# V of batch 3 issued in another pass, the last output tile in two column halves, and a reordered front and first pass, in a chunked attention followed by a snake MLP

## The chip, the cores and the metric

The kernel runs on one core of a Trainium2 chip. The metric is the device time in microseconds of one execution. All work is on that core's engines: PE (TensorE), ACT (ScalarE), DVE (VectorE), POOL (GpSimd) and SP (SyncE), which here only issues DMAs.

## The reference, cut to what matters

Four batches, eight heads, 768 positions, head size 64. Attention is done in chunks of 32 positions, each of which sees 8 memory keys, 16 positions to its left and 8 to its right. The result of all heads is a matrix of 3072 rows and 512 columns, which goes through an MLP with a "snake" in the middle.

```python
# attention, for each chunk c of 32 positions
k_full = concat(mem_k, k[l_start:r_end]);  v_full = concat(mem_v, v[l_start:r_end])
a = softmax(q_c @ k_full.T / sqrt(64));    out[c] = a @ v_full
# MLP on x = out as [3072, 512];  w_in [512, 2048], w_out [2048, 512]
h = x @ w_in
g = h + sin(alpha * h) ** 2 / (alpha + 1e-9)
return g @ w_out
```

## The kernel before, in words

The order of all work is written out by hand; no scheduler moves anything. Each engine has one queue and works through it in the order in which the code issued it.

One batch is a pass of three steps. **Attention** works on eight blocks of 96 positions. `scores` multiplies queries by keys (L283) into a pair of PSUM banks and takes the exponential on ACT (L296). `values` multiplies by V (L309) and divides by the sum on DVE (L315, L316), which gives `x_blk`. The blocks are transposed into `xT`, the first five by DMA on SP's queue (L492), the rest on PE (L326, L329). **`layer`** is the first matrix product: for each of 16 slices `ft` of the hidden width, PE multiplies `w_in` by `xT` (L508, two halves of 384 columns), ACT takes the sine (L528), the square is done by ACT (L532), DVE or POOL (L535) as the letter of a string says (A, V, P), and DVE forms `gT` (L538), which frees the pair of banks. `finish` of a slice is emitted one slice later, or two for a P. **`second`** is the product with `w_out` (L554) into one bank for each 128 rows; `end_o` copies the bank to `o_sb` (two buffers), on DVE (L567) or ACT (L569), and SP sends it out (L570). `second` of one batch is a generator; `feed.take(n)` puts n of its matmuls between the instructions of the next batch's attention and layer. What is left at the end runs alone.

Batches 0 and 1 bring K and Q through PE transposes. For batches 2 and 3, `load_rows(b)` issues 22 DMAs on POOL's queue (L143, L148, L153) that bring rows of K and Q to `kst` and `qst`, with a cast; then SP copies the memory keys (L157) and issues 14 DMA transposes (`cross_steps`, L164 and L167) into `kT` and `qT`. In the layer of batch 1 the rows of batch 2 are loaded, all at its start, behind a small POOL copy that waits for `xT` (`gate`, L719); its 14 transposes stand on SP's queue right behind. In the layer of batch 2 the rows of batch 3 are loaded (gate at L726), and the transposes are issued one for each slice. `load_v(b)` brings V of a batch with two or three POOL DMAs (L183, L200) to one of two buffers `vws`. `send_memv` adds the memory values by SP (L210).

The first attention (`attention_first`) is cut otherwise: by pairs of heads `hp` and halves of the positions. `sc_half` is the scores of one unit (L341 adds the mask, L349 multiplies, L356 exponentiates), `pv` its values (L368, then L374 and L375 on DVE), `x` the transpose to `xT` (L385 on PE, L388 copies on ACT). `warm(n)` issues n matmuls on a tile of zeros (L336) whose result nobody reads; they are written to the bank that the next `x` will use, so they wait for the copy of L388 that read it last. `ahead` begins the first half of slices 0 to 2. At the end of each attention `preload_act_table` makes ACT load the sine's table before it is needed (L460 in the first attention).

Two rules of the order matter for the change. PSUM bank pairs are handed out in a ring: in the first attention `plan(big=(4, 0, 2))` names three pairs, taken in turn by `pv` and `sc_half`; who takes a pair waits for the reader of the one before. And every POOL DMA waits for the one eight before it.

Of the kernel before, what the change touches and what calls it, by code (L numbers as in the profile page):

```python
# [9 lines left out]
P = 128  # L10
# [4 lines left out]
F32 = mybir.dt.float32  # L15
ACTF = mybir.ActivationFunctionType
# [26 lines left out]
def kernel(  # L43
# [12 lines left out]
    nc = tc.nc  # L56
    B, H, S, D = q.shape
    NM = mem_k.shape[2]
    d_model, d_ff = moe_w_in.shape
# [3 lines left out]
    FT = d_ff // P  # L63
    KT = d_model // P
    NSUB = S // P
# [7 lines left out]
    mlp = ctx.enter_context(tc.tile_pool(name="mlp", bufs=3))  # L73
# [4 lines left out]
    ps = psum.tile([P, 8, 512], F32, name="ps")  # L78
# [6 lines left out]
    kept = set()  # L85
# [37 lines left out]
    w_out_sb = consts.tile([P, FT, d_model], BF, name="w_out_sb")  # L123
# [53 lines left out]
    def load_v(b, parts=((0, H),)):  # L177
        vw = vws[b % 2][:].rearrange("p h j c -> p (h j) c")
        flat = v.rearrange("b h s d -> (b h s) d")

        def part(p0, p1, first, c0, c1):
            r0 = S * H * b + QW * c0 + first
            nc.gpsimd.dma_start(  # L183
                vw[p0:p1, c0:c1, 0:D],
                flat[r0:r0 + QW * (c1 - c0)].rearrange("(n t) d -> t n d", t=QW)[0:p1 - p0],
            )

        for h0, h1 in parts:
            c0, c1 = h0 * NJ, h1 * NJ
            if b == 0 and h0 == 0:  # L190
                part(16, 64, 0, 0, 1)
                c0 = 1
            part(0, 64, -16, c0, c1)
            c0, end = h0 * NJ, 0
            if b == B - 1 and h1 == H:
                c1 -= 1
                end = 1
            part(72, 128, 48, c0, c1)
            if end:
                nc.gpsimd.dma_start(vw[72:120, c1, 0:D], flat[B * H * S - 48:B * H * S])  # L200
# [132 lines left out]
    def warm(n):  # L333
        z = ps[:, rings["one"][0], :]
        for _ in range(n):
            nc.tensor.matmul(z, idle[:, 0:P], idle[:])  # L336
# [55 lines left out]
    def attention_first(kq, alphas, ahead):  # L392
        xT = xp.tile([P, KT, S], BF, name="xT")
        pt, xb = {}, {}

        def turn_k(hp):
            t = turn(kq[0], hp, None)
            put_k(0, hp, t)
            put_k_edges(0, hp, t)

        def turn_q(hp):
            put_q(0, hp, turn(kq[1], hp, None))

        def sc_half(hp, half):
            pt[hp, half] = unit_scores(hp, half)

        def sc(hp):
            for half in range(2):
                sc_half(hp, half)

        def pv(*u):
            xb[u] = unit_values(*u, pt[u])

        def x(*u):
            unit_turn(xT, *u, xb.pop(u))

        turn_k(0)
        warm(2)
        turn_q(0)
        mt = packed(single(), HP, 32)  # L420
        for g in range(HP):
            nc.tensor.transpose(mt[:, g, :], memk_bf[0:32, 2 * g:2 * g + 2, :].rearrange("p e d -> p (e d)"), ident[0:32, 0:32])
        nc.vector.tensor_copy(memkT[:], mt)
        put_memk(0)
        warm(3)
        turn_k(1)
        put_memv(0, nc.vector, 0, H)
        warm(2)
        sc(0)
        turn_q(1)  # L430
        alphas()
        warm(3)
        sc(1)
        t2 = turn(kq[0], 2, None)
        put_k(0, 2, t2)
        pv(0, 0)
        put_k_edges(0, 2, t2)
        turn_q(2)
        warm(1)
        pv(0, 1)  # L440
        t3 = turn(kq[0], 3, None)
        put_k(0, 3, t3)
        warm(1)
        x(0, 0)
        sc_half(2, 0)
        put_k_edges(0, 3, t3)
        turn_q(3)
        sc_half(2, 1)
        x(0, 1)
        warm(1)  # L450
        plan(big=(4, 0, 2))
        pv(1, 0)
        sc(3)
        units = [(hp, half) for hp in range(1, HP - 1) for half in range(2)]
        for n in range(1, len(units)):
            pv(*units[n])
            warm(1)
            x(*units[n - 1])
            if n == 1:
                nc.scalar.preload_act_table(ACTF.Sin)  # L460
            warm(1)
        warm(1)
        pv(3, 0)
        x(2, 1)
        pv(3, 1)
        x(3, 0)
        ahead(0, 0, xT)
        ahead(1, 0, xT)
        x(3, 1)
        ahead(2, 0, xT)  # L470
        return xT
# [73 lines left out]
    def second(i, gT, cut=0):  # L545

        def begin_o():
            bank = take_bank("one")
            kept.add(bank)
            return bank  # L550

        def part(s, bank, f0, f1):
            for ft in range(f0, f1):
                nc.tensor.matmul(  # L554
                    ps[:, bank, :], gT[:, ft, P * s:P * s + P], w_out_sb[:, ft, :],
                    start=(ft == 0), stop=(ft == FT - 1),
                )
                if ft < FT - 1:
                    yield

        def end_o(s, bank):
            kept.remove(bank)
            rings["one"].remove(bank)
            rings["one"].append(bank)
            o_sb = mlp.tile([P, d_model], F32, name="o_sb", bufs=2)
            if s % 2 == 0 or state["attending"]:
                nc.vector.tensor_copy(o_sb[:], ps[:, bank, :])  # L567
            else:
                nc.scalar.copy(o_sb[:], ps[:, bank, :])  # L569
            nc.sync.dma_start(out[S * i + P * s:S * i + P * s + P, :], o_sb[:])  # L570

        early = []
        if cut:
            for s in range(2):
                early.append(begin_o())
                yield from part(s, early[s], 0, cut)
        for s in range(NSUB):
            bank = early[s] if s < len(early) else begin_o()
            yield from part(s, bank, cut if s < len(early) else 0, FT)
            end_o(s, bank)  # L580
            yield
# [78 lines left out]
    def layer(i, xT, squares, begin, to_feed):  # L660
        gT = gTs[i % 2]
        pend = []
        fed = 0
        for ft in range(FT):
            begin(ft)
            square = squares[ft % len(squares)]
            squared, fin = first(ft, xT, gT, square, begun.pop(ft, None))
            want = to_feed * (ft + 1) // FT
            feed.take(want - fed)
            fed = want  # L670
            for due, f in [p for p in pend if p[0] <= ft]:
                f()
            pend = [p for p in pend if p[0] > ft]
            squared()
            pend.append((ft + (2 if square == "P" else 1), fin))
        for due, f in pend:
            f()
        feed.add(second(i, gT, 0 if i else 13), NSUB * FT)
# [3 lines left out]
    def begin_0(ft):  # L682
        if ft == 3:
            plan(h=[6] + rings["big"])
        if ft == 11:
            load_v(1)
            send_memv(1)
            send_memv(2)
        if ft == 15:
            prs.extend(pair_up(kq1[n // HP], n % HP) for n in range(4))  # L690

    layer(0, xT, "VPPAPAVPPAPAVAAA", begin_0, 0)
    last4 = rings["h"]
    plan(one=(last4[0], last4[0] + 1), t=(last4[1], last4[1] + 1), big=last4[1:])
    put_memk(1)
# [17 lines left out]
    for i in range(1, B):  # L713
        last = i == B - 1
        crossings = iter(()) if last else cross_steps(i + 1)

        def begin(ft, i=i):
            if i == 1 and ft == 0:
                nc.gpsimd.tensor_copy(gate[:], xT[0:1, 0, QW * 6 - 1:QW * 6])  # L719
                load_rows(2)  # L720
                load_v(3)
                for _ in crossings:
                    pass
            if i == 2:
                if ft == 0:
                    nc.gpsimd.tensor_copy(gate[:], xT[0:1, 0, QW * 6 - 1:QW * 6])  # L726
                    load_rows(3)
                if ft >= 1:
                    next(crossings, None)

        if i == 1:
            assert feed.left() == 16
            plan(h=[min(rings["one"])] + rings["big"])
            layer(i, xT, "VAVAVAVAAVAAVAVA", begin, 0)
            free = rings["h"]
            plan(one=(free[0], free[0] + 1), h=free[1:])
        else:
            plan(h=rings["big"])
            layer(i, xT, "AAAV", begin, feed.left() - (0 if last else 16))
        if not last:  # L740
            plan(big=rings["h"])
            nc.scalar.preload_act_table(ACTF.Exp)
            feed.take(6)
            xT = attention(i + 1, feed, (4, 8, 4, 4, 3, 3, 3, 3, 4, 4, 4), 2, 5)
            if i == 1:
                send_memv(3)
# [31 lines left out]
```

## Time and profile before

| what | value |
|---|---|
| median of 11 runs | 225.65 us (224.01 to 227.31) |
| profiled execution, its own time | 225.86 us |
| its span, first to last instruction | 224.1 us |
| PE busy | 209.1 us, 93% of the span |
| ACT busy, DVE busy, POOL busy | 148.0, 136.0, 82.5 us |
| L554 (`w_out`), one matmul of 512 columns x362 | 94.7 us busy |
| L508 (`w_in`), one matmul of 384 columns x512 | 91.4 us busy |
| granted TensorE clock, mean | 0.997 |

The times in the tables and rows are microseconds from the start of the span; the execution's own time is 1.76 us longer than its span. A row of the timeline gives start, length, engine, line, operation, tiles and, in brackets, the idle time of the engine just before with what ended it. "PEld" is the load of weights, which runs beside PE. "SPq" and "POOLq" are the queues of those engines. A busy PE is not PE at its peak, since the ends of matmuls are modelled.

The stages of the span, by their first rows: first attention to 25.7, layer of batch 0 to 48.2, keys and queries of batch 1 to 60.3, attention of batch 1 to 74.2, its layer to 97.8, attention of batch 2 from 99.2 to 115.8, its layer to 149, attention of batch 3 from 149.2 to 162.9, its layer to 197.7, and the rest of `second` to 219.2.

### The profile page before, as it was taken

To read this page: it belongs to the slowest core of one execution; us is meant where nothing else is said; L and a number is where in the kernel's file an instruction comes from. 1 tells how busy PE (TensorE), PEld (TensorE's weight loads), DVE (VectorE), ACT (ScalarE), POOL (GpSimd) and SP (SyncE) were. 2 spreads that over 40 slices of the span, in tenths; PEclk is the share of its full clock that TensorE was granted. 3 is DMA by queue.
4 is the path that set the end of the run, shared out by engine and by line. 5 is a ranking of instruction groups with operands and counts; after the bars stand their busy time and mean duration, and the time that the engine had idled before them with its cause. 6 is when DMAs were issued, how large, how long until landed. Compare 5 with 4: busy or idle time off the path is not lost.

```text
span 224.1 us, 4352 instructions
## 1 busy us (share of the span) xinstructions
PE 209.1 (93%) x1647; PEld 112.5 (50%) x1672; DVE 136.0 (61%) x233; ACT 148.0 (66%) x217; POOL 82.5 (37%) x102
## 2 busy tenths in 40 slices
PE   7999799999999989999599999999999999999991
PEld 2555555545545545544255555544555555544440
DVE  5866559793437689995563875765845754851110
ACT  2558578994778399998645879797918777741001
POOL 8997663795600799900039960000000000000000
PEclk9999999999999999999999999999999999999998
DMA  5999999999999699999969999642410110112121
GB/s 81 160 170 173 207 207 207 200 173 124 105 174 163 67 170 145 157 156 137 161 110 139 132 109 217 139 119 67 115 52 0 47 50 1 47 47 75 69 94 48
DMA packets 98733, 26.96 MB, mean 120 GB/s; under 512 B 86792, under 2 KB 95640, under 8 KB 98712
## 3 DMA queue, kind: packets, MB, share of 16 engines
q0 software_dynamic: 71520, 14.82, 84.5%
q1 hardware_dynamic: 27192, 11.86, 25.9%
q8 instruction: 13, 0.21, 0.4%
q14 instruction: 8, 0.07, 0.1%
HBM read 29.69 MB, written 6.29 MB: 161 GB/s over the span
## 4 chain that ended last, share of the span: by engine, by line
PE 62%; DMA 10%; POOL 8%; SPq 6%; DVE 5%; ACT 4%; issue 3%; DVEq 0%; ACTq 0%; POOLq 0%
PE ps L554 32%; PE ps L508 23%; DMA kT<-kst 5%; DMA q_bf<-in_q_dram 3%; SPq L164 3%; SPq L167 3%; PE ps L283 2%; DMA qst<-in_q_dram 2%; PE ps L309 2%; DVE gT L538 2%; ACT u L528 2%; POOL kst L148 2%; POOL kst L143 1%; POOL qst L153 1%; POOL vw L183 1%
## 5 line engine op out<-in xcount | busy, mean ns | idle before, releaser
L554 PE MATMUL ps<-w_out_sb,gT 128*128 128x512 bf16 x362 | 94.7, 380 | 1.2
L508 PE MATMUL ps<-xT,w_in_sb 128*128 128x384 bf16 x512 | 91.4, 326 | 2.0 <-DVE gT L538 1.3
L538 DVE SCALAR_TENSOR_TENSOR gT<-u,inv_alpha,ps 128x768 bf16<-128x768 f32 x64 | 63.3, 1012 | 24.1 <-ACT u L532 20.1
L528 ACT ACTIVATE u<-ps,alpha_sb 128x768 f32<-128x768 f32 x64 | 56.7, 896 | 26.7 <-PE ps L508 25.8
L508 PEld LDWEIGHTS <-w_in_sb 128*128 128x128 bf16 x512 | 49.5, 97 | 39.8 <-issue 4.2
L554 PEld LDWEIGHTS <-gT 128*128 128x128 bf16 x384 | 34.3, 97 | 31.4 <-issue 0.9
L532 ACT ACTIVATE u<-u 128x768 f32<-128x768 f32 x40 | 33.7, 843 | 1.3
L296 ACT ACTIVATE pt<-ps,biasm 128x256 bf16<-128x256 f32 x72 | 28.7, 473 | 7.2 <-issue 2.8
L567 DVE COPY o_sb<-ps 128x512 f32<-128x512 f32 x17 | 11.7, 689 | 25.3 <-PE ps L554 24.7
L535 DVE TENSOR_TENSOR u<-u 128x768 f32<-128x768 f32 x18 | 17.2, 953 | 6.0 <-ACT u L528 5.9
L183 POOL DMA_DIRECT2D vw<-in_v_dram x15 | 18.1, 1216 | 0.0
L316 DVE TENSOR_TENSOR x_blk<-ps,rinv 96x512 bf16<-96x512 f32 x24 | 16.5, 686 | 1.1 <-DVE rinv L315 0.3
L569 ACT COPY o_sb<-ps 128x512 f32<-128x512 f32 x7 | 4.1, 584 | 19.0 <-PE ps L554 19.0
L262 ACT COPY kT<-ps 128x672 bf16<-128x672 bf16 x8 | 5.7, 718 | 10.0 <-PE ps L247 5.2
L148 POOL DMA_DIRECT2D kst<-in_k_dram x16 | 11.7, 732 | 0.0
L283 PEld LDWEIGHTS <-kT 64*128 64x128 bf16 x192 | 4.9, 94 | 13.0 <-issue 11.3
L143 POOL DMA_DIRECT2D kst<-in_k_dram x16 | 11.2, 699 | 0.3 <-issue 0.3
L315 DVE RECIPROCAL rinv<-ps 96x8 f32<-96x8 f32 x24 | 4.8, 202 | 10.6 <-PE ps L309 5.4
L336 PE MATMUL ps<-idle 128*128 128x512 bf16 x28 | 9.6, 446 | 1.8 <-DVE vw L596 1.2
L309 PEld LDWEIGHTS <-pt 128*128 128x128 bf16 x192 | 9.0, 98 | 4.1
L283 PE MATMUL ps<-qT,kT 64*128 64x96 bf16 x192 | 8.3, 205 | 3.0 <-DVE o_sb L567 1.3
L153 POOL DMA_DIRECT2D qst<-in_q_dram x12 | 10.8, 903 | 0.0
(77 smaller groups left out, 133.4 us busy)
## 6 DMA issues: line engine op xcount, KB each, us to landing
out_dram<-o_sb SPq DMA_DIRECT2D x24, 256.0 KB
w_out_sb<-in_moe_w_out_dram POOLq DMA_DIRECT2D x2, 1024.0 KB, 18.1
w_in_sb<-in_moe_w_in_dram POOLq DMA_DIRECT2D x3, 512.0 KB, 10.5
vw<-in_v_dram POOLq DMA_DIRECT2D x3, 512.0 KB, 11.8
qst<-in_q_dram POOLq DMA_DIRECT2D x12, 128.0 KB, 4.9
vw<-in_v_dram POOLq DMA_DIRECT2D x2, 448.0 KB, 12.7
kst<-in_k_dram POOLq DMA_DIRECT2D x14, 64.0 KB, 5.0
kst<-in_k_dram POOLq DMA_DIRECT2D x14, 56.0 KB, 4.5
```

The lines of the kernel that those rows point to most:

```text
L148: nc.gpsimd.dma_start(kst[72:72 + n, j, :].rearrange("p (h d) -> p h d", d=D), k[b, :, QW * j + 48:QW * j + 48 + n, :].rearrange("h p d -> ...
L183: nc.gpsimd.dma_start(vw[p0:p1, c0:c1, 0:D], flat[r0:r0 + QW * (c1 - c0)].rearrange("(n t) d -> t n d", t=QW)[0:p1 - p0],)
L283: nc.tensor.matmul(sc[:, e, QW * hp:QW * hp + QW], kTs[b % 2][64 * e:64 * e + 64, hp, pitch * j:pitch * j + P], qTs[b % 2][64 * e:64 * e + ...
L296: nc.scalar.activation(pt[:, 0:H * QW].rearrange("p (g e c) -> p g e c", g=2, e=4)[:, :, :, 32 * m:32 * m + 32], sc[:, :, 0:4 * QW].rearra ...
L309: nc.tensor.matmul(otv[:, e, hp, :], pt[:, QW * i:QW * i + P], vws[b % 2][:, 2 * hp + e, j, 0:D + 1],)
L316: nc.vector.tensor_tensor(out=x_blk[:].rearrange("p g e d -> p e g d"), in0=otv[0:QW, :, :, 0:D], in1=rinv[:].unsqueeze(3).to_broadcast([Q ...
L508: nc.tensor.matmul(hT[:, hf, 0:HALF], w_in_sb[:, kt, P * ft:P * ft + P], xT[:, kt, HALF * hf:HALF * hf + HALF], start=(kt == 0), stop=(kt ...
L528: nc.scalar.activation(u[:], hT[:, :, 0:HALF], ACTF.Sin, scale=alpha_sb[:, ft:ft + 1])
L532: nc.scalar.activation(u[:], u[:], ACTF.Square)
L535: eng.tensor_tensor(out=u[:], in0=u[:], in1=u[:], op=ALU.mult)
L538: nc.vector.scalar_tensor_tensor(out=gT[:, ft, :].rearrange("p (e c) -> p e c", e=2), in0=u[:], scalar=inv_alpha[:, ft:ft + 1], in1=hT[:, ...
L554: nc.tensor.matmul(ps[:, bank, :], gT[:, ft, P * s:P * s + P], w_out_sb[:, ft, :], start=(ft == 0), stop=(ft == FT - 1),)
```

## The change

Four edits. `load_v(3)` goes from the layer of batch 1, behind the rows of batch 2, to the layer of batch 2, between the gate and the rows of batch 3. The last 128 rows of the output are computed as two products of 256 columns, each with its own bank, copy (the first on DVE, the second on ACT) and DMA. In the first attention the scores and values of the units are put in another order, the table load is issued two units earlier in the code, and four of seven `warm` matmuls after `plan(big=(4, 0, 2))` go. In the layer of batch 0 the string of squares becomes "VPPAPAVPAVPPAAAA" (POOL squares slices 10 and 11 where it had 8 and 10; DVE 9 where it had 12; ACT 8 and 12 where it had 9 and 11), and `load_v(1)` is issued at slice 12 where it was 11, which puts it behind the last POOL square as before.

```diff
         plan(big=(4, 0, 2))
         pv(1, 0)
-        sc(3)
+        sc_half(3, 0)
+        pv(1, 1)
+        sc_half(3, 1)
         units = [(hp, half) for hp in range(1, HP - 1) for half in range(2)]
-        for n in range(1, len(units)):
+        x(1, 0)
+        nc.scalar.preload_act_table(ACTF.Sin)
+        for n in range(2, len(units)):
             pv(*units[n])
-            warm(1)
+            if n == 2:
+                warm(2)
             x(*units[n - 1])
-            if n == 1:
-                nc.scalar.preload_act_table(ACTF.Sin)
-            warm(1)
         warm(1)
         pv(3, 0)
         x(2, 1)
...
+        def halves(s):
+            for hf in range(2):
+                bank = begin_o()
+                c = slice(256 * hf, 256 * hf + 256)
+                for ft in range(FT):
+                    nc.tensor.matmul(
+                        ps[:, bank, 0:256], gT[:, ft, P * s:P * s + P], w_out_sb[:, ft, c],
+                        start=(ft == 0), stop=(ft == FT - 1),
+                    )
+                    if ft % 2 == 1 and (hf == 0 or ft < FT - 1):
+                        yield
+                kept.remove(bank)
+                o_sb = mlp.tile([P, d_model], F32, name="o_sb", bufs=2)
+                (nc.vector.tensor_copy if hf == 0 else nc.scalar.copy)(o_sb[:, 0:256], ps[:, bank, 0:256])
+                nc.sync.dma_start(out[S * i + P * s:S * i + P * s + P, c], o_sb[:, 0:256])
...
         for s in range(NSUB):
+            if i == B - 1 and s == NSUB - 1:
+                yield from halves(s)
+                yield
+                break
...
-        if ft == 11:
+        if ft == 12:
             load_v(1)
             send_memv(1)
             send_memv(2)
...
-    layer(0, xT, "VPPAPAVPPAPAVAAA", begin_0, 0)
+    layer(0, xT, "VPPAPAVPAVPPAAAA", begin_0, 0)
...
             if i == 1 and ft == 0:
                 nc.gpsimd.tensor_copy(gate[:], xT[0:1, 0, QW * 6 - 1:QW * 6])
                 load_rows(2)
-                load_v(3)
                 for _ in crossings:
                     pass
             if i == 2:
                 if ft == 0:
                     nc.gpsimd.tensor_copy(gate[:], xT[0:1, 0, QW * 6 - 1:QW * 6])
+                    load_v(3)
                     load_rows(3)
```

The order of SP's queue is the same after the change, but for the last tile's two DMAs in place of one. On POOL's queue the three DMAs of V stand behind the gate of batch 2's layer where they stood ahead of it. All lines below are those of the kernel before.

## The prediction, as it was put on record

> **What bounds the kernel now.** I read the page first. PE is busy 209.1 of 224.1 us and carries most of the chain of waits, so time is won only where PE stands still, or where it works at nothing. The granted clock is full in every slice. Then the chain of waits in order of time, for the places where it leaves PE:
>
> ```profile
> 21.39 0.40 ACT xT L388
> 21.81 1.28 ACT L460
> 23.11 0.49 ACT xT L388
> 23.64 0.59 PE ps L336 x2
> 24.76 0.70 DVE x_blk L375
> ...
> 101.99 10.22 DMA kT<-kst
> 112.26 0.34 PE ps L283 x8
> ...
> 208.47 10.75 PE ps L554 x49
> 219.29 0.59 ACT o_sb L569
> ```
>
> The reader is to see three places. In the first attention the chain runs through a table load on ACT. Near 102 it runs for 10.22 us through one DMA transpose of batch 2's keys. At the end it runs through the copy of the last tile and its DMA. The change touches all three.
>
> The middle one is the largest. PE's timeline in the attention of batch 2, blocks 5, 6 and 7:
>
> ```profile
> 107.06 0.34 PE L283 MATMUL ps<-qT,kT 64*128 64x96 bf16 x8
> 109.71 0.35 PE L283 MATMUL ps<-qT,kT 64*128 64x96 bf16 x8 [1.31 <-DVE o_sb L567]
> 112.26 0.34 PE L283 MATMUL ps<-qT,kT 64*128 64x96 bf16 x8 [1.20 <-DMA kT<-kst]
> ```
>
> The same three in the attention of batch 3, which has the same order:
>
> ```profile
> 156.81 0.34 PE L283 MATMUL ps<-qT,kT 64*128 64x96 bf16 x8
> 158.09 0.34 PE L283 MATMUL ps<-qT,kT 64*128 64x96 bf16 x8
> 159.36 0.34 PE L283 MATMUL ps<-qT,kT 64*128 64x96 bf16 x8
> ```
>
> Batch 2 needs 2.65 and 2.55 us from block to block, batch 3 needs 1.28 and 1.27. The difference is 1.37 + 1.28 = 2.65 us. The first stall is put down to a copy of `o_sb`, but in batch 3 block 6 ran at 158.09, before the like copy (158.68), and nothing in `scores` reads it. In the compiled order the weight load of block 6 waits for two DMA transposes, those of its keys and of the last queries, so I take both stalls for late transposes. Why are they late?
>
> SP's and POOL's queues in the timeline:
>
> ```profile
> 100.64 1.24 SPq L167 DMA_TRANSPOSE qT<-qst  x1
> 101.99 1.23 SPq L164 DMA_TRANSPOSE kT<-kst  x1
> ```
>
> ```profile
> 90.18 0.66 POOL L148 DMA_DIRECT2D kst<-in_k_dram  x1
> 90.81 3.36 POOL L183 DMA_DIRECT2D vw<-in_v_dram  x2
> ```
>
> SP had issued the last queries by 101.88 and the last keys by 103.22; block 6 got them at 109.7 and block 7 at 112.25, some 8 and 9 us later. The DMA view says what shared the engines: the two large parts of V of batch 3, issued at 90.81 and 92.4, landed 12.4 and 20.7 us later, at 103.2 and 113.1. With nothing large in flight a transpose is quick: in batch 1's attention SP had issued the fourth of the `xT` transposes near 73.0, and PE, which needs four of them, went on at 74.21 after a wait of 0.23.
>
> **The change part by part. V of batch 3.** It leaves the stretch from 90.8 to 113.1. The rows of batch 2 have landed by 97.0 (last issue 90.18 plus 6.8), so from then on only transposes and output are in flight, and the last two should land within 1 to 4 us, at 103 to 107. They are needed at 108.3 and 109.6 when the stalls are gone. Gain 2.65 us; bounds 0 (the lateness is the transposes' own) and 2.65, and I take 2.65, because batch 3 shows the same code without the stall.
>
> Where it goes it moves work too. POOL passes the gate at 115.56. Three V issues (1.66 + 1.70 + 0.56) now stand ahead of 22 row issues, so the first row goes out at 120.0 where it was 116.08. V needs 14.0 us from first issue to last landing where it runs alone (batch 2: issued 56.43, landed 65.1 and 70.4) and 14.9 for batch 1, so it ends at 130 to 131, and the first rows land just behind it at some 131.5. Also the sixth to eighth row DMAs wait for the DMA eight before them, which are now V's parts, so POOL stops and issues the keys of block 2 at some 130.5 instead of 120.7, the last row at 142. Then SP, whose order is unchanged: its first transpose starts at 129.04 (held by the memory keys' DMA) and the last at 147.80, nearly back to back. It would start at 131.5 to 133 and end near 152. Block 7 of batch 3 needs the last one at 159.36. With 1.2 us for landing there are 6 us to spare, with the 9 us that batch 2 showed it is 1.7 late. Rows and V have landed by then, so I take 0 and keep 0 to 1.7 for the range. The output DMAs on SP behind those transposes move by 3 us; their `o_sb` buffers are wanted at 148.0, 152.2 and 158.7, after they land. V itself is needed at 153.28. All these times move alike when the gain ahead of them comes, so the margins stand.
>
> **The last tile.** 32 matmuls of 256 columns for 16 of 512. The trace gives 219 ns for 512 columns (10.75 us for 49) and 167 for 384 (16.07 for 96), so 0.405 ns a column and 115 ns at 256: 3.69 - 3.51 = +0.18 us. [...] I take the trace's +0.18. The copy on ACT falls from 0.59 to an estimated 0.37 (the same kind of copy takes 0.48 for 384 columns and 0.80 for 768, so 0.83 ns a column): -0.21. SP waits 2.4 us for the last DMA; the DMA's share in the windows shows its bytes from 220.6 to 221.4, the rest is start and completion, so half the bytes save some 0.4, bounds 0 and 0.8. The first half's copy and DMA lie beside the second half's matmuls. The ACT copy must wait for the DMA of the tile before, issued at 216.51 and by the last one's 2.7 us done at 219.2; it is ready at 219.4. Sum -0.4 us, bounds 0 and -0.8.
>
> **The front.** The path is the one shown: exponential, copy of xT(1,0), table load 1.28, copy of xT(1,1), a filler matmul that waits for this copy, `pv(3,0)`, DVE, `x(3,0)`, L508. Removing four fillers of 0.22 us wins nothing by itself, since PE waits 0.46 ahead of 23.64 anyway; two of those behind the wait become one, which is -0.22. But `pv(1,1)` now stands ahead of `sc_half(3,1)`, and this one takes the bank that DVE frees at 20.19. Its mask matmul starts at 20.25 where it was 19.76, so the exponential, the table load and the copy are late by 0.47. DVE gets `pv(1,1)` 0.7 us sooner and its next units with it, but this ends in the same wait. Sum +0.25 us; bounds -0.5 (ACT catches up) and +0.5.
>
> **Layer of batch 0.** Letters stay 6 P, 3 V and 7 A, so busy times stay. PE waits 0.15 us at 48.19 for `gT` of slice 12 (a V that ends at 48.13). As an A it ends earlier by my walk through the queues: -0.15. The last `gT` comes 0.4 later (51.57 to 52.0), under 20 matmuls that last till 52.67. POOL ends its last square 1.5 us later, so V of batch 1 is issued at 45.7 instead of 44.12 and lands by 60.6, needed at 64.82; the first `pr` copy ends at 49.9, needed at 52.3. SP's memory values wait for their own source DMA until 42.38 and do not move. If these covers were gone each costs up to 1 us. I take -0.15, bounds -0.3 and +0.3.
>
> **Sum.** -2.65 - 0.4 + 0.25 - 0.15 = -2.95. Against the profiled execution, 225.86, of which 224.1 are span: 222.9. That execution lies 0.2 above the median of the runs shown, so the median becomes 222.7.
>
> **The rivals.** A. The gain comes, with the front and tail anywhere within their bounds: 221.6 to 223.9. Chance 0.72.
>
> B. Only part of it: the late transposes are partly their own (SP's 14 back to back), or batch 3's last block waits 1 to 1.7 us. For it speaks that transposes and rows together kept landings at 6 us and more even before V was issued; against it that batch 3 has no stall with the same 14. 224 to 225.4, taken at 224.4. Chance 0.16.
>
> C. Slower. V in front of the rows sets the end of batch 3's transposes. If V takes the 22.3 us that it took in batch 2's rows (90.81 to 113.1), its end is 138.4, SP starts at 139 and ends 10 us late, at 159; with 2 to 5 us for landing block 7 waits 2 to 5 us and the blocks before it take their share. It decides from the point where SP's first transpose starts more than some 7 us late. At 5 us the sum is 227.7. Against it: V's 22.3 us were spent beside transposes, and here it goes first. Chance 0.08.
>
> D. The clock. [...] Chance 0.04, mostly within 0.5% of no change.
>
> **How the numbers follow.** A change of 0.5% is 1.13 us, about what a measurement of this kernel can tell from none: faster means under 224.5, slower over 226.8. All of A and half of B are faster, 0.80; half of B, D and a little of C make 0.13; the rest of C and what I have not seen, 0.07. The likeliest is 222.7. The range takes A whole and most of B, 221.6 to 224.7.
>
> **What would show it.** After: block 6 and 7 of batch 2 at 1.3 us from the ones before, without a wait; L164's first row in batch 3's layer at 131 to 133 and no wait at L283 in batch 3; the table load at about 22.3 and L508's first row near 25.9; SP's last wait near 2.0. The prediction is wrong if L283 of batch 2 still waits, if batch 3's L283 does, or if PEclk falls below 1.00 near 24.

## The result, and the profile after

| | before | after |
|---|---|---|
| median | 225.53 us (47 runs) | 222.50 us (12 runs, 221.37 to 224.13) |
| ratio of the times, 95% interval | | 0.9893 [0.987, 0.9917] |
| profiled execution, its own time / its span | 225.86 / 224.1 us | 222.49 / 220.7 us |

The change saves 1.1%. The forecast was 222.7, in the range 221.6 to 224.7. Taken stage by stage, the two profiled spans differ like this:

| stage, from first row to first row | before | after | difference |
|---|---|---|---|
| start to `pv(1,0)`, ahead of anything changed | 18.83 | 19.26 | +0.43 |
| `pv(1,0)` to the first `w_in` product | 6.85 | 7.14 | +0.29 |
| from there to the first `w_out` product | 22.51 | 22.40 | -0.11 |
| attention of batch 2, first scores to first `w_in` product | 16.65 | 14.32 | -2.33 |
| the same of batch 3 | 13.73 | 13.72 | -0.01 |
| start of the last ACT copy to the end of the span | 4.81 | 3.27 | -1.54 |
| the rest, by subtraction | | | -0.13 |
| span | 224.1 | 220.7 | -3.4 |

The first row is not the change's: other executions of both fronts start `pv(1,0)` anywhere between 18.49 and 19.28. Read it as the size of what one execution can add by itself.

The new lines sit above the old ones in the code, so L508, L554, L492, L460, L567 and L570 of before are now L510, L556, L494, L458, L569 and L572; the two halves of the last tile are L579 to L588. PE in the attention of batch 2, blocks 5 to 7 and the first product behind them:

```profile
107.55 0.34 PE L283 MATMUL ps<-qT,kT 64*128 64x96 bf16 x8
108.82 0.34 PE L283 MATMUL ps<-qT,kT 64*128 64x96 bf16 x8
110.10 0.34 PE L283 MATMUL ps<-qT,kT 64*128 64x96 bf16 x8
...
113.98 0.81 PE L510 MATMUL ps<-xT,w_in_sb 128*128 128x384 bf16 x4 [0.15 <-DMA xT<-x_blk]
```

Blocks 6 and 7 follow at 1.27 and 1.28 us with no bracket: both waits are gone. The new bracket, 0.15 us for `xT`, shows what is late next. The layer's first product now waits for the transposes of `xT`, which before had finished in the shadow of the stall. From block 7 to that product it was 3.56 us and is 3.88, so 0.32 us of the gain is lost here.

The front, in the chain of waits:

```profile
21.48 0.81 ACT pt_first L356
22.29 0.37 ACT xT L388
22.68 1.28 ACT L458
23.97 0.49 ACT xT L388
```

The same chain as before, through the same table load. The exponential at its head ends 3.03 us behind `pv(1,0)` (22.29 - 19.26), where it was 2.56 before (21.39 - 18.83): the 0.47 us of the prediction. On ACT the table load stands where it stood, between the copies of `xT(1,0)` and `xT(1,1)`; the text on the change is wrong to say that it was issued two units earlier. In PE's timeline the filler at 24.50 carries the wait:

```profile
24.50 0.38 PE L336 MATMUL ps<-idle 128*128 128x512 bf16 x1 [1.11 <-ACT xT L388]
```

POOL and SP around the place where V went:

```profile
113.90 3.36 POOL L183 DMA_DIRECT2D vw<-in_v_dram  x2 [0.32 <-issue]
...
117.79 0.68 POOL L143 DMA_DIRECT2D kst<-in_k_dram  x1
...
122.73 0.89 POOL L153 DMA_DIRECT2D qst<-in_q_dram  x1 [1.25 <-DMA vw<-in_v_dram]
128.18 0.69 POOL L143 DMA_DIRECT2D kst<-in_k_dram  x1 [4.55 <-DMA vw<-in_v_dram]
```

```profile
123.75 0.69 SPq L157 DMA_DIRECT2D kst<-memk_st  x1
131.18 1.21 SPq L164 DMA_TRANSPOSE kT<-kst  x1
...
150.04 1.21 SPq L164 DMA_TRANSPOSE kT<-kst  x1
```

V goes out first, POOL stops 5.8 us in all behind its parts, and SP's transposes of batch 3 run from 131.18 to 150.04. In this execution batch 3's first product (161.07) carries no wait.

The tail, in the timeline, and below it what SP waited for:

```profile
213.74 3.66 PE L579 MATMUL ps<-w_out_sb,gT 128*128 128x256 bf16 x32
215.74 0.42 DVE L587 COPY o_sb<-ps 128x256 f32<-128x256 f32 x1 [1.11 <-PE ps L579]
216.19 1.97 SPq L588 DMA_DIRECT2D out_dram<-o_sb  x2
217.43 0.37 ACT L587 COPY o_sb<-ps 128x256 f32<-128x256 f32 x1 [6.32 <-PE ps L579]
```

```profile
SPq L795 <- DMA out_dram<-o_sb: 1.1, 1, 1.1
```

The first half leaves at 216.19, while PE still works on the second. The last copy takes 0.37 us for 0.59, and SP's last wait is 1.1 us where it was 2.4.

### The profile page after: what moved, and what is told of

The parts are those of the page before. It is cut to its first block, busy times and chain, and to the rows that moved or that the text cites. A ratio compares the mean times of both kernels' runs of the same rounds, so it can differ in the third digit from the quotient of the medians.

```text
span 220.7 us, 4387 instructions
## 1 busy us (share of the span) xinstructions
PE 209.1 (95%) x1659; PEld 114.1 (52%) x1684; DVE 136.8 (62%) x234; ACT 147.8 (67%) x217; POOL 82.8 (38%) x102
## 4 chain that ended last, share of the span: by engine, by line
PE 74%; DVE 12%; ACT 6%; issue 3%; DMA 2%; POOL 1%; DVEq 0%
PE ps L556 33%; PE ps L510 26%; DVE gT L540 5%; PE ps L336 3%; DVE u L537 3%; PE ps L283 3%; ACT u L530 2%; PE ps L309 2%; DMA xT<-x_blk 2%; PE ps L579 2%; PE ps L247 1%; PE ps L326 1%; DVE x_blk L375 1%; PE ps L244 1%; DVE qT L269 1%
## 5 line engine op out<-in xcount | busy, mean ns | idle before, releaser
L510 PE MATMUL ps<-xT,w_in_sb 128*128 128x384 bf16 x512 | 91.4, 326 | 2.2 <-DVE gT L540 1.3
L556 PE MATMUL ps<-w_out_sb,gT 128*128 128x512 bf16 x346 | 91.3, 380 | 1.1
L510 PEld LDWEIGHTS <-w_in_sb 128*128 128x128 bf16 x512 | 49.4, 97 | 40.3 <-issue 5.0
L556 PEld LDWEIGHTS <-gT 128*128 128x128 bf16 x368 | 32.7, 97 | 29.2 <-issue 0.5
L569 DVE COPY o_sb<-ps 128x512 f32<-128x512 f32 x17 | 11.7, 689 | 25.3 <-PE ps L556 24.7
L537 POOL TENSOR_TENSOR u<-u 128x768 f32<-128x768 f32 x6 | 9.2, 1544 | 7.6 <-ACT u L530 7.6
L571 ACT COPY o_sb<-ps 128x512 f32<-128x512 f32 x6 | 3.5, 584 | 12.7 <-PE ps L556 12.7
L336 PE MATMUL ps<-idle 128*128 128x512 bf16 x24 | 9.0, 497 | 2.5 <-DVE vw L618 1.2
```

The costliest lines, as they stand in the source:

```text
L510: nc.tensor.matmul(hT[:, hf, 0:HALF], w_in_sb[:, kt, P * ft:P * ft + P], xT[:, kt, HALF * hf:HALF * hf + HALF], start=(kt == 0), stop=(kt ...
L537: eng.tensor_tensor(out=u[:], in0=u[:], in1=u[:], op=ALU.mult)
L556: nc.tensor.matmul(ps[:, bank, :], gT[:, ft, P * s:P * s + P], w_out_sb[:, ft, :], start=(ft == 0), stop=(ft == FT - 1),)
```

## The experiments

Twelve kernels ran, four to a chip. Every ratio is to the kernel before on the same chip: its medians there were 225.17 us (the first four), 224.81 (the second) and 224.62 (the third). "Stretch of the front" means `pv(1,0)` to the first `w_in` product, "batch 2" and "batch 3" the two attention stretches of the table above.

### The change in parts

**V alone.** The kernel before, with only this:

```diff
                 load_rows(2)
-                load_v(3)
...
+                    load_v(3)
                     load_rows(3)
```

> The kernel before with the move of V of batch 3 alone. Theory (V's transfer held up the last transposes of batch 2): from block 0's L283 to the first L508 of the layer the attention of batch 2 shrinks from 16.65 us by 2.3, as in the changed kernel (14.32), blocks 6 and 7 wait for nothing, and the time falls by 2.3 to 2.7 us (ratio 0.988 to 0.990). Rival 1 (the change as a whole is worth 3.0 us mostly by its other parts; the tail alone showed 1.5 in one profile): V alone gives 1.5 us or less. Rival 2 (V in front of the rows makes batch 3 wait): L283 of batch 3 waits, and the gain is under 1 us.

Measured: 224.5 us, 0.9975 [0.9954, 0.9996]. Batch 2 shrank to 14.50 us in the profile and its score waits are gone, but batch 3 grew to 15.06. PE there, last block and first product:

```profile
157.57 0.34 PE L283 MATMUL ps<-qT,kT 64*128 64x96 bf16 x8
162.47 0.81 PE L508 MATMUL ps<-xT,w_in_sb 128*128 128x384 bf16 x4 [1.18 <-DMA xT<-x_blk]
```

and SP ahead of it:

```profile
151.87 1.21 SPq L164 DMA_TRANSPOSE kT<-kst  x1
...
154.34 5.09 SPq L492 DMA_TRANSPOSE xT<-x_blk  x4
```

The scores never waited in batch 3. What V pushed late is the end of SP's queue: the last key transpose goes out at 151.87, and the transposes of `xT` stand in order behind it, at 154.34, 6.93 us after this batch's first scores (147.41). In the profile of the changed kernel they start 6.09 us after them (153.44 and 147.35). So in this profile the move wins 2.15 us in batch 2 and loses 1.33 of it in batch 3. The time of all executions shows less still, 0.56 us (0.09 to 1.04), so the forecast of 2.65 us for this part is not met.

**The tail alone.** The kernel before, with `halves` for the last tile of the last batch and nothing else:

```diff
         for s in range(NSUB):
+            if i == B - 1 and s == NSUB - 1:
+                yield from halves(s)
+                yield
+                break
```

> The kernel before with the last tile in two column halves alone. From the start of the last copy on ACT to the end of the span it was 4.81 us before and 3.27 in the changed kernel, where the prediction's terms (copy -0.21, DMA -0.4) allow 4.2. Theory A (half the bytes in the last DMA end its slow remainder): the stretch is 3.3 again, SP's last wait near 1.1 instead of 2.4, and the time falls by 1.0 to 1.5 us. Theory B (the 2.4 us of the profile before was one execution's slow DMA): the time falls by 0.4 to 0.6 us. PE: the last tile's matmuls end no later than before (0 to 0.04 us), where the prediction had +0.18.

Measured: 223.57 us, 0.9935 [0.9912, 0.9958], a gain of 1.5 us where the prediction's sum had 0.4. From the last copy to the end of the span it is 3.31 us. (In the profiled execution the granted clock was 0.76 from 110 to 115, in batch 2's stall, so its whole span isn't compared.) SP's last wait is again 1.1 us.

**The front alone.** The kernel before, with the new order of `sc_half(3, 0)`, `pv(1, 1)`, `sc_half(3, 1)`, the load and the fillers, and nothing else:

```diff
         pv(1, 0)
-        sc(3)
+        sc_half(3, 0)
+        pv(1, 1)
+        sc_half(3, 1)
...
+        x(1, 0)
+        nc.scalar.preload_act_table(ACTF.Sin)
...
-            if n == 1:
-                nc.scalar.preload_act_table(ACTF.Sin)
```

> The kernel before with the new order of the first attention alone (units, table load, fillers; squares of batch 0 as before). Theory (the table load stands on the path and starts later): from pv(1,0)'s first L368 to the first L508 it takes 7.14 us as in the changed kernel where it was 6.85 before, so the time rises by 0.2 to 0.3 us, ratio 1.001, which the measurement can't tell from none. Rival (the new order saves, and what the changed profile lost it lost at the start): the stretch is 6.8 or less and the time falls.

Measured: 225.78 us, 1.0037 [1.0012, 1.0061]. The stretch of the front is 7.15 us, 0.30 longer. This part of the change costs time. The profile also names the first stall of batch 2 for what it is; with V in its old place, blocks 6, 7 and the product behind them:

```profile
109.55 0.35 PE L283 MATMUL ps<-qT,kT 64*128 64x96 bf16 x8 [0.91 <-DMA qT<-qst]
111.06 0.34 PE L283 MATMUL ps<-qT,kT 64*128 64x96 bf16 x8 [0.17 <-DMA kT<-kst]
...
116.04 0.81 PE L510 MATMUL ps<-xT,w_in_sb 128*128 128x384 bf16 x4 [1.25 <-DMA xT<-x_blk]
```

Block 6 waits for the transposed queries here, as it does with the cut transfer and with batch 0's layer alone (1.35 and 2.02 us), and not for the copy of `o_sb` that the profile of before named. And the stall moves: what is not lost at blocks 6 and 7 is lost at the product, and the whole stretch is 16.63 us.

**All but the front.** The changed kernel with the front of before, so that diff read backwards:

```diff
         pv(1, 0)
-        sc_half(3, 0)
-        pv(1, 1)
-        sc_half(3, 1)
+        sc(3)
```

> The changed kernel with the first attention's order of before put back. Theory: 0.3 us faster than the changed kernel, 222.2 where that has 222.5, stretch from pv(1,0) to the first L508 6.85 us. Rival: 0.2 to 0.5 us slower.

Measured: 222.76 us, 0.99 [0.9857, 0.9942]. The stretch of the front is back at 6.86 us, but batch 2's and batch 3's first products waited 0.42 and 0.43 us for `xT` and ate this in the profile (span 221.0 against 220.7). The interval is too wide to say more.

**Batch 0's layer alone.** The kernel before, with two edits:

```diff
-        if ft == 11:
+        if ft == 12:
...
-    layer(0, xT, "VPPAPAVPPAPAVAAA", begin_0, 0)
+    layer(0, xT, "VPPAPAVPAVPPAAAA", begin_0, 0)
```

> The kernel before with only batch 0's layer changed: the new order of the squares and V of batch 1 issued one step later. Theory (the stall at the first output product, 0.47-0.63 us at L554 in three of the four profiles with the old order, 0.15 in the fourth, is what this edit removes): the stretch from the first Sin to the first L554 falls to 22.4 from 22.5-22.98, whole -0.3 to -0.6 us, ratio 0.997-0.9985. Rival 1 (as the prediction had it, -0.15 us): ratio 0.999-1.0, not told from none. Rival 2: the later V of batch 1 costs a wait in batch 1's attention: ratio above 1.001.

Measured: 224.16 us, 0.9983 [0.9965, 1.0001]. The interval just takes in one, so a gain in time is not shown. The profiles are plainer: from the first `w_in` to the first `w_out` product it takes 22.39 us here. The old order took 22.51 in before's profile and in that of V ahead of the rows (below), with a wait of 0.15 us for `gT`, but 22.82 to 23.00 in four others, with waits of 0.47 to 0.64. The new order took 22.38 to 22.40 in five profiles at full clock and 22.76 in a sixth (V in the middle of the rows), with a longer wait earlier in the layer.

### Where V may stand

**V ahead of the rows in batch 1's pass.** The kernel before, with `load_v(3)` one line higher, ahead of `load_rows(2)`. This is the mechanism of the prediction's rival C, tried where the rows have less time.

```diff
+                load_v(3)
                 load_rows(2)
-                load_v(3)
```

> The kernel before with the load of batch 3's V left in batch 1's pass but put ahead of batch 2's rows there. It asks what V ahead of rows costs where the rows are needed at once. Theory (rival C of the prediction: V's 3.9 us of issue[...] hold the rows back, then SyncE's transposes): the first L164 of this pass goes from 83.1 to 89-93, the last from 102 to 108-113, and batch 2's attention waits 5 to 9 us more in blocks 0 to 7; whole 230-234 us. Rival (the pass has slack, as batch 3's has): the last L164 stays under 104 and the attention stretch is 16.2-16.9 as before; whole 225 plus or minus 1.

Measured, one execution: 229.3 us, span 227.5. The first L164 of this pass is at 90.11 and the last at 109.99, as the theory had it. PE in batch 2:

```profile
103.68 0.35 PE L283 MATMUL ps<-qT,kT 64*128 64x96 bf16 x8 [0.92 <-DMA qT<-qst]
106.78 0.34 PE L283 MATMUL ps<-qT,kT 64*128 64x96 bf16 x8 [1.54 <-DMA kT<-kst]
109.63 0.35 PE L283 MATMUL ps<-qT,kT 64*128 64x96 bf16 x8 [1.29 <-DMA qT<-qst]
111.51 0.41 PE L283 MATMUL ps<-qT,kT 64*128 64x96 bf16 x8 [0.54 <-DMA qT<-qst]
```

Four blocks in a row wait, and the stretch is 20.30 us for 16.65. The 3.65 us more are less than the 5 to 9 expected, and not all of them are V's: the granted clock was 0.67 from 110 to 115, around the last of these waits, where it is 1.00 in before's profile. Rival C is a real mechanism all the same. In the change the first transpose goes out 16.2 us ahead of the first scores (131.18 and 147.35), here 9 us (90.11 and 99.06); that this margin is what kept the scores of batch 3 from waiting is argued, not tested.

**V behind the rows in batch 2's pass.** The changed kernel, with `load_v(3)` one line lower:

```diff
-                    load_v(3)
                     load_rows(3)
+                    load_v(3)
```

> The changed kernel with V of batch 3 still in batch 2's pass, but behind batch 3's rows. Theory (the order inside this pass is what makes the rows, and so the xT transposes, late: POOL waits 5.8 us[...] between rows): no such POOL waits, the first L164 near 127 instead of 131, the last near 146-148, no xT wait in batch 3, and V, issued near 131-135, lands before batch 3's first use near 148: 0 to -0.6 us against the changed kernel, 221.9-222.5. Rival: V lands after its first use and the probability products of batch 3 wait 0.5 to 3 us for it: 223-225.5.

Measured: 222.82 us, 0.9914 [0.9894, 0.9934], not told from the changed kernel. POOL did not stop and the first L164 went out at 128.00, 13.24 us behind the layer's first product where it is 17.20 in the changed kernel. But the last one came only at 149.56, and nothing had been waiting for it: batch 3 takes 13.73 us in both profiles. So the order of V and rows inside this pass makes no difference that these runs can tell. That V has left the pass before does: batch 2 takes 14.41 us here too.

**The memory values later.** The changed kernel, with batch 3's memory values moved on SP:

```diff
                     load_v(3)
                     load_rows(3)
+                    send_memv(3)
...
-            if i == 1:
-                send_memv(3)
```

> The changed kernel with the eight copies of batch 3's memory values (L210, 5.96 us of SyncE's queue) moved behind the memory keys' copy (L157) in the same layer pass. Theory (the keys' transposes of batch 3 start late because the memory keys' copy is issued at 123.75, behind these eight, and lands 6.6 us later among V's traffic): L157 is issued near 117.5-118, the first L164 stands at 124-125.5 instead of 131.18, the last one 2 to 6 us earlier than 150.04, and no xT wait is left in batch 3 (0.43 and 1.18 us in the runs with V alone and with the old front, 0 in the profile after); whole 0 to -0.8 us against the changed kernel, about 222.1. Rival: the rows' landing behind V sets the start; the first L164 stays within 1.5 us of 131, the last within 1 us of 150, and the time is the changed kernel's.

Measured: 223.01 us, 0.9896 [0.9858, 0.9935]. The theory fell. L157 went out at 117.78 as it said, yet the first transpose came 15.66 us behind the layer's first product, where it was 17.20 in the changed kernel, and not the 6 us or so earlier that was expected:

```profile
117.78 0.73 SPq L157 DMA_DIRECT2D kst<-memk_st  x1
...
130.88 1.22 SPq L164 DMA_TRANSPOSE kT<-kst  x1
```

```profile
SPq L164 <- DMA kst<-in_k_dram: 4.2, 1, 4.2
```

With the memory keys out of the way SP waits for the key rows themselves. In the changed kernel the wait was put down to the memory keys' copy (6.6 us). V ahead of the rows is what delays them: with V behind them (above) the first transpose came at 13.24 us by the same measure.

### The table load

**The load later.** The changed kernel, with one line moved:

```diff
         x(1, 0)
-        nc.scalar.preload_act_table(ACTF.Sin)
...
         x(3, 0)
+        nc.scalar.preload_act_table(ACTF.Sin)
```

> The changed kernel with one line moved: the load of the Sin table on ScalarE (1.28 us, 22.68 in the profile after) is issued after the row group x(3,0) instead of before the last two xT copies. Theory (the front loses because the load now sits between the copies of xT(1,0) and xT(1,1), and the next products wait for that copy, 1.11 us at L336 in the profile after): the stretch from pv(1,0) to the first Sin product shrinks from 7.14 us to 5.9-6.2, the whole by 0.9 to 1.3 us, to about 221.5 us; ratio to the kernel before near 0.983. Rival 1: the load is on the path to the first Sin wherever it stands, because the first Sin itself needs it: the stretch stays at 7.1 plus or minus 0.2, ratio as the changed kernel's 0.989. Rival 2: VectorE's rows (rinv, x_blk) end just behind the copy and take over the wait: a gain of 0.3 us or less.

Measured: 220.86 us, 0.9815 [0.978, 0.9851], the fastest kernel of the study beside the next one. PE and ACT in the timeline:

```profile
23.69 0.48 ACT L388 COPY xT<-ps 128x384 bf16<-128x384 bf16 x1 [0.35 <-PE ps L385]
24.38 0.34 PE L385 MATMUL ps<-ident,x_blk 96*128 96x96 bf16 x4 [0.48 <-DVE x_blk L375]
24.56 1.70 PE L510 MATMUL ps<-xT,w_in_sb 128*128 128x384 bf16 x8
...
25.26 1.28 ACT L468 ACT_TABLE_LOAD   x1
```

The load of 1.28 us now runs beside the first products of the layer, which wait for nothing that ACT has still to do. The stretch of the front is 5.87 us (24.56 - 18.69), 1.27 less than in the changed kernel and 0.98 less than before; the clock has a part in the rest of the gain (below). Both rivals, the load needed at once and VectorE taking over the wait, are out.

**Both.** The late load and the late memory values together, that is both diffs:

```diff
+                    send_memv(3)
...
         x(3, 0)
+        nc.scalar.preload_act_table(ACTF.Sin)
```

> The changed kernel with both edits of the runs on the table load and on the memory values together. If each does what its theory says: 222.5 - 1.1 - 0.4 = about 221.0 us, ratio 0.981. If the late table load gains nothing: 222.1, ratio 0.987. If both gain nothing: 222.5, ratio 0.989.

Measured: 220.83 us, 0.9814 [0.978, 0.9848]: the late load's time, and nothing from the memory values.

**The load later, V in the middle of the rows.** As the late load, with `load_v(3)` called inside `load_rows(3)`, at its fourth step:

```diff
-                    load_v(3)
-                    load_rows(3)
+                    load_rows(3, lambda: load_v(3))
...
-    def load_rows(b):
+    def load_rows(b, mid=None):
         for jt in order:
             j = jt[0]
+            if mid is not None and j == 3:
+                mid()
```

> The kernel with the late table load (220.86 us), with V's load put in the middle of batch 3's rows (ahead of the fifth row group) instead of ahead of them. Theory (the first transposes start late only because V's parts stand ahead of the first rows): first L164 6 to 7 us after the memory keys' copy falls to 3-4, near 126-127 instead of 129.8, last one no later than 148.8; whole 0 to -0.5 us against that kernel. Rival: V's bytes have to be moved somewhere and the last rows now come later: last L164 at 149-151, xT waits of 0.4-1.2 us in batch 3, whole 0 to +1.0.

Measured: 221.02 us, 0.9837 [0.98, 0.9874]. The first transpose is at 126.61 and the last at 147.66, as expected, and the time does not move, since with the late load alone batch 3 took 13.72 us already.

### The tail's transfer

**One tile, two transfers.** The kernel before, with one copy of the last tile and its transfer cut into two of 256 columns:

```diff
-            nc.sync.dma_start(out[S * i + P * s:S * i + P * s + P, :], o_sb[:])
+            if i == B - 1 and s == NSUB - 1:
+                for c in (slice(0, 256), slice(256, 512)):
+                    nc.sync.dma_start(out[S * i + P * s:S * i + P * s + P, c], o_sb[:, c])
+                return
+            nc.sync.dma_start(out[S * i + P * s:S * i + P * s + P, :], o_sb[:])
```

> The kernel before, with only the last output tile's transfer cut: one product and one ScalarE copy of 512 columns as before, then two transfers of 256 columns each (128 KB) from it. Theory A (the tail of the kernel before is the time that the last 256 KB take to land, 2.4 us of SyncE's last wait against 1.1 with halves): the two transfers share the landing no better than one, since the bytes behind the last copy are the same; SyncE's last wait stays at 2.0-2.6, the second issue adds 0 to 0.5; whole 225.2, ratio 0.998 to 1.003. Theory B (it is the form of the transfer, longer rows or one queue's share of the engines, that makes the 256 KB slow): the wait falls to 1.1-1.5 and the whole gains 0.6 to 1.2 us, ratio 0.995-0.997. With the two-halves change measured at 0.9935, Theory A leaves that gain to the first half's early copy and departure.

Measured: 224.64 us, 1.0001 [0.9974, 1.0027]: no gain in the time, as theory A has it, though SP's last wait was shorter than it said, 1.6 us in two pieces. From the end of the last copy to the end of the span it is 3.87 us here. Five executions with one transfer of 256 KB gave 4.22, 4.10, 3.32, 4.11 and 4.29; eight with halves gave 2.85 to 2.95. So cutting the transfer alone shows no gain. What pays is that the first half is computed, copied and on its way before the second is ready, with 128 KB left behind the last copy.

## Why the prediction was right, and where it wasn't

| term | predicted | the two profiles | the part alone, from its ratio |
|---|---|---|---|
| V | -2.65 | -2.34 | -0.56 (-1.04 to -0.09) |
| last tile | -0.4 | -1.54 | -1.46 (-1.98 to -0.95) |
| front | +0.25 | +0.29 | +0.83 (+0.27 to +1.37) |
| layer of batch 0 | -0.15 | -0.11 | -0.38 (-0.79 to +0.02) |
| sum | -2.95 | -3.27 with the start's +0.43, -3.70 without | -1.57 |
| the whole | | -3.4 | -2.41 (-2.93 to -1.87) |

The last column is one minus the ratio, times the median of the kernel before on that chip, with the ends of the interval. "The two profiles" gives V the sum of batch 2's and batch 3's rows. The median of 222.5 hits the forecast of 222.7, but in part by luck: V alone was worth far less than its term, and the last tile more.

**V: right in mechanism, too large in size.** The stalls at blocks 6 and 7 are late transposes, and they go when V leaves the pass. The four profiles with V in its old place that are compared here (before, the front alone, the cut transfer, batch 0's layer alone) have 16.65, 16.63, 15.66 and 16.28 us in batch 2; the eight with V moved have 14.24 to 14.59, mean 14.40. That makes 1.9 us. V alone, in the time of all executions, gained 0.56, and even the upper end of its interval, 1.04, is under half of the term. So for V itself it was rival B, a part of the gain, that came nearest. The step that was off is that the whole 2.65 of one profile would be kept: 0.3 us comes back because `xT` is late next, and up to 1.3 in batch 3. The prediction looked there for block 7's keys, with 6 us to spare, and passed over the `xT` transposes, which have to wait in the same queue on SP. Two of the eight profiles show that wait in batch 3 (1.18 and 0.43 us), both with the old front and both on one chip; the runs do not tell these two apart.

**Batch 3's start: right.** L164 at 131 to 133 was 131.18, and no score waits there. The last one came at 150.04 instead of 152.

**The last tile: the DMA was mis-sized.** Its bounds of 0 to 0.8 us do not hold the measured 1.3 (from the copy's end to the span's, 4.22 to 2.90). The prediction halved only the bytes seen in the windows. But the wait behind 256 KB is longer by more than the bytes, 4.1 to 4.3 us in four profiles and 3.3 in a fifth, while behind 128 KB it is the same to 0.1 us in eight. Why is not shown. The copy came as said (-0.22). For PE the prediction took 115 ns a product, +0.18 us. In the traces the starts of the last tile's products lie 216 ns apart with 512 columns and 109 ns with 256, which is +0.04 us. The 219 ns that the prediction read from 10.75 us for 49 products are too long, since a row's length also holds the whole last product (0.38 us) and not only the step to the next.

**The front: right on the path, and one cost was priced at nothing.** +0.25 was +0.29 and +0.30. Yet the front alone cost 0.8 us in time. The rest is rival D, the clock, for which the prediction has a chance of 0.04 and no term in its sum. The sign that it named, a clock under 1.00 near 24, is absent from the profile after, but two profiles of kernels with the same front show it.

In the profiles of V behind the rows and of the late memory values the granted clock was half for a while at the start of the layer. For each of the two, the rows give the 3.41 us ahead of this and then the stretch itself, for the second in three pieces whose ends also hold some time at full clock. The last row is the 3.41 us of the front in which PE works least in the changed kernel:

```profile
core 0: us, PE busy (x) PEld busy (x) DVE busy (x) ACT busy (x) POOL busy (x), PEclk, DMA share, GB/s
21.57:24.98 3.41, 1.85 (x38) 1.38 (x35) 1.93 (x5) 2.88 (x5) 3.01 (x4) 1.00 1.28 206
24.98:28.39 3.41, 2.93 (x13) 1.55 (x14) 1.22 (x3) 0.54 (x2) 0.60 (x2) 0.50 1.24 206
...
22.50:25.91 3.41, 1.61 (x30) 1.24 (x31) 1.90 (x5) 2.19 (x4) 2.59 (x4) 1.00 1.24 203
25.60:26.00 0.40, 0.39 (x6) 0.29 (x7) 0.37 (x2) 0.01 (x1) 0.00 (x0) 0.89 1.23 205
26.00:28.00 2.00, 2.00 (x8) 0.99 (x7) 0.39 (x1) 0.47 (x1) 0.60 (x1) 0.50 1.24 205
28.00:30.00 2.00, 2.00 (x13) 1.22 (x12) 0.00 (x0) 0.48 (x1) 0.55 (x1) 0.67 1.24 206
...
22.80:26.21 3.41, 1.39 (x26) 1.03 (x25) 1.93 (x6) 2.50 (x4) 2.33 (x3) 1.00 1.25 208
```

PE was busy for 1.85 and 1.61 us of the 3.41 ahead, with no single wait longer than 1.12 us, and then the clock was 0.50 for 3.41 us each time, from 24.98 and from 25.91, just as the layer's products began. In the changed kernel's profile PE was busy for only 1.39 us of the 3.41, and the clock stayed at 1.00 there and behind. So PE's busy time ahead does not tell by itself whether the clock falls, and what decides it is not shown. With the two other fronts PE works more: at the least 2.26 of 3.40 us in before's profile (23.00 to 26.40) and 2.57 with the late load (22.00 to 25.40), and the clock is 1.00 in both.

The mean granted clock of each execution shows how many pay: 4 of the 12 runs of the changed kernel have 0.990 to 0.992, and their median is 223.7 us against 222.4 for the other eight, 1.3 us more. With V behind the rows it is 11 of 22 (223.2 against 222.2), with the late memory values 4 of 7 (223.5 against 221.7), with the front alone 11 of 22 (226.4 against 225.4; some of these may lie in batch 2's stall). In that stall the clock fell too: in the profile of the tail alone it was 0.76 from 110 to 115, behind a wait of 2.37 us. On that chip 7 of 56 executions of the kernel before have 0.985 to 0.992, and none of 22 with V alone. With the late load it is none in 17 runs of three kernels (0.997 or more). For the front alone, half of the runs at 1.0 us more and 0.3 for the path come to the 0.8 us that were measured.

**Batch 0's layer: right in sign, under-sized.** The prediction could save only the 0.15 us of stall that before's profile had. Four of six profiles of the old order have 0.47 to 0.64.

**The total.** That the sum was near is luck in part: the tail gained 1.1 us more than said, and V and the clock gave back about as much. The parts measured alone add up to 1.57 us and the whole gives 2.41; against the intervals of the four parts that is not a difference.

## What to carry to other kernels

When a transfer is moved out of one queue, walk the queue behind its new place to the end, to the work of the next stage that stands in it too, and not only to the first thing that might wait. Size a stall by several profiles, and with what it hides: one showed 2.65 us at two blocks, but in four the move was worth 1.9 us of the stretch on average, and less in time. And the table load that stood between two copies on the path cost its full length here, 1.28 us, while behind them it cost nothing: that line was worth 1.27 us of the front, and none of 17 executions with it showed the fall of the clock.

## What the runs showed of the hardware

- In two profiles the granted clock was 0.50 for 3.41 us at the start of batch 0's layer, although no single wait of PE in the front is longer than 1.12 us; in the 3.41 us ahead PE was busy for 1.85 and 1.61 us. In the changed kernel's profile it stayed at 1.00 around 3.41 us with 1.39 us of busy PE. Only part of the executions of the same kernel show a lower mean clock (4 of 12, 11 of 22, 4 of 7 and 11 of 22), and they took 1.0 to 1.7 us more by the medians.
- From the last copy to the end of the span it took 3.3 to 4.3 us behind one transfer of 256 KB, and 2.85 to 2.95 behind one of 128 KB. The bytes at the rate seen in the windows (358 to 410 GB/s) explain 0.3 us of that.
- Products of 512 columns started 216 ns apart and those of 256 columns 109 ns apart in the last tile, so cutting the tile cost PE 0.04 us.
